# Two layers of an SSM convolution and a GEGLU FFN: another order of passes, half visits at the handover, and block 1's transform by tokens mod 4

## The chip, the cores and the metric

The kernel runs on one core of a Trainium2 chip. The metric is the device time of one execution in microseconds, and less is better. In the names below PE is the matmul engine (TensorE), DVE the VectorE, ACT the ScalarE, POOL the GpSimd and SP the SyncE, whose queue issues most DMAs; PEld are PE's weight loads.

## The reference

```python
def _A_ref(q, k, v, shift_k, ssm_k, ssm_D):          # B=1, S=2048, D=576
    k_shift = sum over t<4 of k_pad[:, t:t+S, :] * shift_k[:, 3-t]
    kv = k_shift * v
    y  = causal convolution of kv with ssm_k along S   # rfft of length 2S in the reference
    return q * (y + kv * ssm_D)

def _B_ref(x, w_gate, w_up, w_down):                  # F=4608
    return (_gelu(x @ w_gate) * (x @ w_up)) @ w_down

x = A_q
x = x + _A_ref(_layernorm(x), A_k, A_v, A_shift_k, A_ssm_k, A_ssm_D)
x = x + _B_ref(_layernorm(x), B_w_gate, B_w_up, B_w_down)
x = x + _A_ref(_layernorm(x), A_k, A_v, A_shift_k, A_ssm_k, A_ssm_D)
x = x + _B_ref(_layernorm(x), B_w_gate, B_w_up, B_w_down)
```

Two layers share all weights. The convolution works on `k` and `v` alone, so its result `y` is the same in both layers; only the gate `q` differs.

## The kernel before

**Units, passes, visits.** The 2048 tokens are four chunks of 512 (`CH`), a chunk four rows of 128 tokens. A unit is one layer of one chunk, numbered 0 to 7: (0,0), (0,1), (1,0), (1,1), (0,2), (0,3), (1,2), (1,3), as (layer, chunk). `passes` (L810) lists which units go through the FFN together. A pass runs three phases `ph` (`NP`), each over 12 of the 36 tiles of 128 features, and in each phase visits its units in turn, so that the units of a pass share one load of the weights. A visit of a unit has two parts. First, for each of 12 tiles, 18 matmuls `gu` (L1103): nine blocks of 64 rows of the contraction, `gate` weights on the upper half of PE's rows and `up` weights on the lower half, 512 columns each. Then the `down` product `dn` (L1768), 192 matmuls of 64 rows and 288 columns that add four rows of tokens, two rows at a time (`two_rows`).

**Evictions.** A tile's PSUM bank is emptied in one of two ways: ACT does the gelu (L1700) and DVE multiplies it with `up` from PSUM (L1701); or, when there is much work for DVE, ACT does the gelu (L1691) and a copy of `up` (L1692), and DVE multiplies the two from SBUF (L1693). The product is `hT`, which `dn` reads. Three PSUM banks go round among `gu` and `dn` tiles; the fourth, `cps`, belongs to the convolution, which may borrow one of the three.

**Handover.** After the last phase of a unit in layer 1 each row goes through a chain: sum into `x_c` with the row's total (L1798), mean on POOL (L933), sum of squares on ACT (L941), `rstd` on POOL (L949), the factor `yh` from `y` on ACT (L977), the gate on DVE (L987), again mean, squares and `rstd`, the norm `xn` on DVE (L1016, L1018), and two DMA transposes on SP (L1058) into `xnT`, the moving operand of the next unit's `gu`.

**The convolution.** Class `Conv` transforms blocks of 512 tokens of `kv` and of the filter, multiplies them (`prod`) and transforms back (`inverse`) into `y[m]`, needed by chunk m. Blocks 2 and 3 are transformed in quarters, by tokens mod 4 (`fwd4`, `quarter`, 288-column matmuls `cps` at L310); block 1 by `fwd` and `fwd_h`, with twice as many matmuls. These are put between the matmuls of the FFN.

**Order.** The order of every engine is fixed when the program is built. A planner (`Pace` with the costs `C_..`, `fill`, `run_v`, `run_vq`, `run_aq`, `run_p`) keeps an estimate of each engine's clock and fills the convolution and the handover in beside the visits' work. Weights are loaded by SP in its program order: `load_wgu` (L869 to L877, three DMAs for one set of four tiles; three buffers) and `load_wd` (L879 to L885; three buffers). `when_due` gives each a due time, and `weights` issues it up to `SOON` = 30 us ahead, but only `HOLD` = 14 us ahead while rows wait for their norm or transposes. A load waits on SP until its buffer has been read, and what stands behind it waits too.

Of the kernel before, what the change touches and what calls it, by code (L numbers as in the profile page):

```python
# [10 lines left out]
ACT = mybir.ActivationFunctionType  # L11
# [22 lines left out]
C_P0, C_P1, C_AC = 1.28, 1.35, 0.7  # L34
C_TT, C_ST, C_BN, C_NORM, C_HT, C_GELU, C_EVA, C_EVD, C_YH = 0.74, 0.80, 0.47, 0.62, 0.615, 0.51, 0.56, 0.72, 0.7
C_HB = 0.345
C_FOLD = 0.46
# [3 lines left out]
SLOW, PRESS = 5.0, 22.0  # L41
# [93 lines left out]
class Conv:  # L135
# [9 lines left out]
    def __init__(self, tc, ctx, pace, gwork, xtp, A_k, A_v, A_shift_k, A_ssm_k, A_ssm_D, ident, cps, ypool):  # L145
# [22 lines left out]
        self.nT = self.cst.tile([P, 5, P], BF16, name="nT")  # L168
        self.V_ = self.cst.tile([P, 2, RT, P], BF16, name="V")
        self.nV = self.cst.tile([P, 3, P], BF16, name="nV")  # L170
# [124 lines left out]
    def fwd_eo(self, src, kt, s, h, ring, scale=1.0):  # L295

        nc = self.nc
        ps = yield from self.both_steps(lambda ps: [ps[:, e, 0:HW] for e in range(2)],
                                   [([self.fw(kt, s, i + e) for e in range(2)],
                                     [src(i + e)[:, h * HW:(h + 1) * HW] for e in range(2)]) for i in (0, 2)])  # L300
        eo = self.eo_tile(ring)
        nc.scalar.activation(out=eo[:], in_=ps[:, :, 0:HW], func=ACT.Copy, scale=scale)
        return eo

# [16 lines left out]
    def quarter(self, src, e, s, h, scale=1.0):  # L321
# [5 lines left out]
        eo = self.eop.tile([P, 2, HW], F32, tag="eo", name="eo")  # L327
# [3 lines left out]
    def cross(self, eo, lo, hi):  # L331
        for dst, op in ((lo, ALU.add), (hi, ALU.subtract)):
            self.nc.vector.tensor_tensor(out=dst, in0=eo[:, 0, :], in1=eo[:, 1, :], op=op)

# [59 lines left out]
    def step(self, m, kv=None, loaded=False):  # L394
# [74 lines left out]
        def fwd(kt, s, h):  # L469
            def run():  # L470
                if s == 0 and h == 0:
                    for k in (kt, kt + 2):
                        kc[k] = self.kcp.tile([P, 2, D], BF16, tag="kc", name="kc")
                free, ring = self.eo_free(True)
                self.eo_at[ring].popleft()
                cur = self.cur
                eo = yield from self.fwd_eo(lambda i: self.vt_[m][:, i, :], kt, s, h, ring)
                done = t.on_act(C_EVA, max(t.pe + 0.25 + LAG, free))
                self.ps_free[cur] = done
                if (kt, s, h) == (1, 1, 1):  # L480
                    self.fwd_at[m] = t.pe + 0.25
                cols = slice(h * HW, (h + 1) * HW)

                def fin():
                    self.cross(eo, kc[kt][:, s, cols], kc[kt + 2][:, s, cols])
                    when = t.on_dve(2 * C_BF, done + LAG)
                    self.eo_at[ring].append(when + LAG)
                    mark(("kc", kt, s, h), when + LAG)
                    if s == 1 and h == 1 and m < self.NB - 1:
                        for k in (kt, kt + 2):  # L490
                            self.spill(self.Kd[m][k], kc[k], when + LAG)
                self.U.append((done + LAG, 2 * C_BF, fin))
            return run

        hh = self.hh if m == 1 else {}

        def fwd_h(kt, s, h):
            def run():
                if (kt, s, h) == (0, 0, 0):
                    self.hh_tiles()  # L500
                free, ring = self.eo_free(True)
                self.eo_at[ring].popleft()
                cur = self.cur
                eo = yield from self.fwd_eo(self.ht[m], kt, s, h, ring, 1.0 / NFQ)
                done = t.on_act(C_EVA, max(t.pe + 0.25 + LAG, free))
                self.ps_free[cur] = done
                if (kt, s, h) == (1, 1, 1):
                    self.hf_at[m] = t.pe + 0.25
# [1361 lines left out]
```

## Time and profile before

| | before |
|---|---|
| median of 3 runs | 909.99 us (909.66 to 910.07) |
| span of the profiled execution (no device time of its own is listed for it) | 907.9 us |
| what the median has beyond that span | 2.1 us |
| PE busy | 902.9 us, 99% of the span |
| DVE, ACT, POOL busy | 556.8, 364.5, 142.0 us |
| DMA | 129.73 MB, mean 143 GB/s |

The profile is one execution, taken by the hardware profiler. Its page gives busy times and shares; a busy PE says little, since matmuls are pipelined and their ends modelled. The chain that ended last is followed back from the last instruction, step by step to what released it. A group of instructions has one row: its line, engine, operation, tile written <- tiles read, shapes and count, then busy us and mean ns, then the idle time before. A DMA's landing is counted from its issue. In a table by stretches of time, the columns after PE, PEld, DVE, ACT and POOL are PE's granted clock, the mean busy share of the DMA engines, and GB/s.

### The profile page before, as it was taken

How to read it: one execution, taken by the hardware profiler on the slowest of the kernel's cores; microseconds unless marked ns; L12 is line 12 of the kernel's file. 1: busy time of each engine (PE TensorE's matmuls, PEld its weight loads, DVE VectorE, ACT ScalarE, POOL GpSimd, SP SyncE). 2: the span in 40 equal slices, each digit the busy share in tenths (PEclk: the TensorE clock that was granted, in tenths of full speed). 3: DMA queues.
4: the chain of work that ended last, by engine and by line, in shares of the span. 5: the costliest groups of instructions: out<-in, count | busy, mean ns of one | idle time of the engine just before them, and what ended most of it. 6: DMA issues, size and time to landing. Idle time of an engine off the chain costs nothing.

```text
span 907.9 us, 24267 instructions
## 1 busy us (share of the span) xinstructions
PE 902.9 (99%) x10465; PEld 601.3 (66%) x10465; DVE 556.8 (61%) x1109; ACT 364.5 (40%) x677; POOL 142.0 (16%) x311
## 2 busy tenths in 40 slices
PE   9999999999999999999999999999999999999998
PEld 7757656577576675775766766757757657667666
DVE  8898988654789876667888744553333334433332
ACT  7784446625434356354244233451121224321211
POOL 5423003320113012230023001220000002100000
PEclk9999999999999999999999999999999999999999
DMA  9999967877519503974934702762720820777630
GB/s 242 314 265 285 231 143 137 179 232 135 170 56 258 128 3 67 270 201 102 251 120 123 167 14 69 138 124 63 136 79 3 157 80 14 142 178 179 135 102 28
DMA packets 128272, 129.73 MB, mean 143 GB/s; under 512 B 43298, under 2 KB 120483, under 8 KB 128164
## 3 DMA queue, kind: packets, MB, share of 16 engines
q1 hardware_dynamic: 119138, 93.22, 47.7%
q0 software_dynamic: 8880, 34.36, 11.0%
q8 instruction: 82, 1.34, 0.6%
q10 hardware_dynamic: 146, 0.59, 0.2%
q14 instruction: 26, 0.21, 0.1%
HBM read 106.91 MB, written 11.80 MB: 131 GB/s over the span
## 4 chain that ended last, share of the span: by engine, by line
PE 98%; POOL 0%; ACT 0%; issue 0%; DVE 0%; ACTq 0%
PE gu L1103 61%; PE dn L1768 30%; PE cps L310 2%; PE ps L284 2%; PE dn L1729 1%; PE ps L1344 0%; PE ps L1103 0%; PE ps L1479 0%; POOL rstd L1564 0%; PE ps L1257 0%; PE ps L1315 0%; PE cps L373 0%; PE ps L278 0%; ACT yh L1526 0%; PE ps L1373 0%
## 5 line engine op out<-in xcount | busy, mean ns | idle before, releaser
L1103 PE MATMUL gu<-xnT,wgu 64*128 64x512 bf16 x5148 | 561.4, 376 | 0.0
L1103 PEld LDWEIGHTS <-wgu 64*128 64x128 bf16 x5220 | 293.2, 94 | 260.6 <-issue 0.7
L1768 PE MATMUL dn<-wd,hT 64*128 64x288 bf16 x4512 | 293.9, 283 | 0.0
L1768 PEld LDWEIGHTS <-hT 64*128 64x128 bf16 x4512 | 254.4, 94 | 26.2
L1700 ACT ACTIVATE ga<-gu 128x512 f32<-128x512 f32 x175 | 104.4, 597 | 311.0 <-PE gu L1103 307.8
L1701 DVE TENSOR_TENSOR hT<-ga,gu 128x512 bf16<-128x512 f32 x175 | 120.1, 687 | 167.5 <-ACT ga L1700 167.3
L1691 ACT ACTIVATE ga<-gu 128x512 bf16<-128x512 f32 x111 | 66.2, 597 | 149.9 <-PE gu L1103 143.9
L1693 DVE TENSOR_TENSOR hT<-ga 128x512 bf16<-128x512 bf16 x112 | 47.0, 421 | 59.6 <-ACT ga L1692 59.5
L1692 ACT CAST ga<-gu 128x512 bf16<-128x512 f32 x111 | 64.3, 579 | 0.0
L933 POOL TENSOR_SCALAR means<-s 128x1 f32<-128x1 f32 x28 | 10.4, 372 | 248.7 <-DVE x_c L1798 219.4
L1804 DVE SCALAR_TENSOR_TENSOR x_c<-dn,means,x_c 128x576 f32<-128x576 f32 x28 | 22.8, 815 | 28.4 <-PE dn L1768 28.4
L1806 DVE TENSOR_TENSOR x_c<-x_c,dn 128x576 f32<-128x576 f32 x32 | 24.1, 752 | 25.8 <-PE dn L1768 25.5
L949 POOL TENSOR_TENSOR rstd<-ve,neghalf_t 128x1 f32<-128x1 f32 x56 | 35.4, 632 | 4.7
L345 DVE TENSOR_TENSOR prod<-prod 128x576 bf16<-128x576 bf16 x64 | 29.3, 458 | 2.2
L328 ACT ACTIVATE eo<-cps 128x576 f32<-128x576 f32 x32 | 20.8, 651 | 23.5 <-PE cps L310 17.3
L1785 DVE TENSOR_TENSOR xn<-x_c,dn 128x576 bf16<-128x576 f32 x15 | 11.3, 754 | 26.5 <-PE dn L1768 24.2
L656 DVE TENSOR_TENSOR kc<-ab,cd 128x288 bf16<-128x288 f32 x64 | 25.3, 452 | 0.0
L443 POOL DMA_DIRECT2D kr<-Kd x20 | 11.2, 558 | 88.2 <-DVE prod L344 88.2
L941 ACT ACTIVATE junk<-x_c,nm 128x576 bf16<-128x576 f32 x28 | 21.5, 769 | 2.2 <-POOL nm L933 1.6
L977 ACT ACTIVATE yh<-y,rstd 128x576 f32<-128x576 bf16 x28 | 21.4, 768 | 1.1 <-POOL rstd L949 1.1
L448 POOL DMA_DIRECT2D hr<-Hd x32 | 17.8, 556 | 24.1 <-DVE prod L344 22.6
L948 POOL TENSOR_SCALAR ve<-ss 128x1 f32<-128x1 f32 x56 | 13.9, 248 | 43.7 <-ACT junk L941 43.4
(177 smaller groups left out, 626.4 us busy)
## 6 DMA issues: line engine op xcount, KB each, us to landing
wgu<-in_B_w_gate_dram SPq DMA_DIRECT2D x45, 576.0 KB, 5.9
wd<-in_B_w_down_dram SPq DMA_DIRECT2D x30, 864.0 KB, 7.1
wgu<-in_B_w_up_dram SPq DMA_DIRECT2D x45, 512.0 KB, 7.5
hr<-Hd POOLq DMA_DIRECT2D x32, 288.0 KB, 4.6
kr<-Kd POOLq DMA_DIRECT2D x24, 288.0 KB, 3.9
Kd<-kc POOLq DMA_DIRECT2D x12, 288.0 KB, 6.4
k<-in_A_k_dram POOLq DMA_DIRECT2D x3, 1008.0 KB, 10.3
wgu<-in_B_w_up_dram SPq DMA_DIRECT2D x45, 64.0 KB, 7.3
```

The source lines that it names most:

```text
L345: nc.vector.tensor_tensor(out=dst[:, cols], in0=pr[:, 0, cols], in1=pr[:, 1, cols], op=ALU.subtract if part == 0 else ALU.add)
L656: nc.vector.tensor_tensor(out=into[k][:, plane, cols], in0=a, in1=b, op=op)
L949: nc.gpsimd.tensor_tensor(out=v["rstd"][:], in0=ve[:], in1=neghalf_t[:, 0:1], op=ALU.pow)
L1103: nc.tensor.matmul(cols(pair[:, s, :]), lhsT=w[r0:r0 + HK, k, gi * P:(gi + 1) * P], rhs=cols(xnT[r0:r0 + HK, blk_of[k], :]), start=(k == 0 ...
L1691: nc.scalar.activation(out=ga[:, 0, :], in_=pair[:, 0, :], func=ACT.Gelu_apprx_tanh)
L1692: nc.scalar.copy(out=ga[:, 1, :], in_=pair[:, 1, :])
L1693: nc.vector.tensor_tensor(out=hT[:, fi, :], in0=ga[:, 0, :], in1=ga[:, 1, :], op=ALU.mult)
L1700: nc.scalar.activation(out=ga[:], in_=pair[:, 0, :], func=ACT.Gelu_apprx_tanh)
L1701: nc.vector.tensor_tensor(out=hT[:, fi, :], in0=ga[:], in1=pair[:, 1, :], op=ALU.mult)
L1768: nc.tensor.matmul(acc[:, g, 0:HW], lhsT=lhs[r], rhs=wn[r, g * HW:(g + 1) * HW], start=step == 0 and fi == 0, stop=step == 1 and fi == FP - 1)
L1804: nc.vector.scalar_tensor_tensor(out=xh, in0=acc[:, :, 0:HW], scalar=m_[:, 0:1], in1=xh, op0=op, op1=ALU.add)
L1806: nc.vector.tensor_tensor(out=xh, in0=xh, in1=acc[:, :, 0:HW], op=ALU.add)
```

## The change

Passes go `[0], [2], [1], [3, 4], [5, 6], [7]` in place of `[0], [1, 2], [3, 4], [5, 6], [7]`: chunk 0 does both its layers first, then chunk 1 alone does layer 1, then its layer 2 with chunk 2. That makes six passes of three phases, so the weights are loaded six times and not five. The last visit of layer 1 and the first of layer 2 of chunks 0 and 1 (`SPLIT`) are done in halves of 256 tokens: 12 tiles of `gu` with 256 columns, the `dn` of two rows, then the same for the other two rows. The first half of the layer-2 visit needs only two rows of `xnT`. Block 1 goes through `fwd4` like the other blocks, on both rings of `eo` tiles; `fwd`, `fwd_h` and `fwd_eo` are gone. The products of the convolution are split into multiplications and a later `join`. Square sums write to one persistent `junk`, the negated planes `nT`, `nV` go to a pool of the start, transposes may be issued up to `SPREAD` = 2 us ahead of the planned norm, and the preparation of a row moves to other visits.

```diff
-    passes = [[0], [1, 2], [3, 4], [5, 6], [7]]
+    passes = [[0], [2], [1], [3, 4], [5, 6], [7]]
     NWB = len(passes) * NP
+    at_once = [units.index((1, c)) for c in range(2)]
+    SPLIT = {(units.index((0, c)), NP - 1) for c in range(2)} | {(n, 0) for n in at_once}
...
+        if ui in at_once:
+            return tasks + [norm(i) for i in range(j - 1, j + 1) if j % 2]
         lag = 2 if layer == 0 else 1
...
     def spreads(now=False, tensor=False):
-        while xn_made and (now or xn_made[0][3] <= t.pe):
+        while xn_made and (now or xn_made[0][3] <= t.pe + (SPREAD if xn_made[0][0] == coming[0] and t.pe > due_at[0] - PRESS else 0.0)):
...
-            if conv_first:
+            if conv_first and not pressing():
...
-        at_start = {(0, 0): [("es", 1), ("prep", 1)], (1, 0): [("x", 2)], (2, 1): [("es", 2)],
+        at_start = {(0, 0): [("es", 1)], (2, 1): [("prep", 1)], (1, 0): [("x", 2)], (1, 1): [("es", 2)],
...
+            split = (ui, ph) in SPLIT
...
+            inputs(RT // 2 if split else RT)
...
+            def features(part=None):
+                ahead[0] = NEVER
+                conv.alt = None
+                last = final and part != 0
+                size = 1.0 if part is None else 0.5
+                cols = (lambda a: a) if part is None else (lambda a: a[:, part * CH // 2:(part + 1) * CH // 2])
...
+                for fi in range(FP):
+                    n, gi = divmod(wb * FP + fi, FG)
+                    w = wgu[n]
...
+                        pair = pr("gu")
+                        gu(pair, w, gi, cols, xnT)
...
+                    if gi == FG - 1 and last:
+                        when_due(t.pe + (FP - FG) * C_GU + 12.0, load_wgu, n + 3)
...
+            for part in range(2) if split else (None,):
+                if part == 1:
+                    inputs(RT)
+                if part != 0:
+                    begin()
...
+                features(part)
...
+                for j in (0, 2) if part is None else (2 * part,):
+                    rows(j)
...
         def steps(filt, ready):
-            limit = lambda: max(ready(), 0.0 if self.eo_at["eo"] else NEVER)
-            if m > 1:
-                for h in range(2):
-                    for e in range(2):
-                        for s in range(2):
-                            self.Pq.append((limit, 0.25, fwd4(filt, e, s, h)))
-                return
-            for kt in range(2):
-                for s in range(2):
-                    for h in range(2):
-                        self.Pq.append((lambda: max(
-                            ready(), 0.0 if self.eo_at["eo"] or self.eo_at["yh"] else NEVER), 0.49, (fwd_h if filt else fwd)(kt, s, h)))
+            limit = lambda: max(ready(), 0.0 if self.eo_at["eo"] or m == 1 and self.eo_at["yh"] else NEVER)
+            for h in range(2):
+                for e in range(2):
+                    for s in range(2):
+                        self.Pq.append((limit, 0.25, fwd4(filt, e, s, h)))
...
+    def mul(self, part, K, H, pr):
+        nc = self.nc
+        if part == 0:
+            nc.vector.tensor_tensor(out=pr[:], in0=K[:], in1=H[:], op=ALU.mult)
+        else:
+            for s in range(2):
+                nc.vector.tensor_tensor(out=pr[:, s, :], in0=K[:, s, :], in1=H[:, 1 - s, :], op=ALU.mult)
+
+    def join(self, part, pr, dst):
+        self.nc.vector.tensor_tensor(out=dst, in0=pr[:, 0, :], in1=pr[:, 1, :], op=ALU.subtract if part == 0 else ALU.add)
...
+        def products(kt, items):
...
+            steps = [(ready(items[n][0]), C_M1 if items[n][1] else C_M0, mult(n)) for n in reversed(range(len(items)))]
+            return steps, (now, len(items) * C_BF + 0.02, join)
```

More of the change, by code (lines that the diff above doesn't have):

```diff
@@ L40 @@
 AHEAD = 2.0
-SLOW, PRESS = 5.0, 22.0
+SLOW, PRESS, SPREAD = 5.0, 22.0, 2.0
 NAT, NEAR = 22.0, 2.2
@@ L467, in step @@
                            load(kt, a)))
[L469 to L493, printed above, removed]
@@ L542, in fin, with join @@
                         if a < m:
                             self.kr_free[kr[(kt, a)][0]] = when
-                return fin
-            return run
+                    return fin
+                return run
+            def join():
+                for n in reversed(range(len(items))):
+                    a, part = items[n]
+                    dst = hr[(kt, a)][1][:, part, :] if own else tiles[len(items) - 1][:, n, :]
+                    self.join(part, tiles[n], dst)
+                    prs[part, a, kt] = dst
+                return lambda when: None
```

297 lines of the change are left out of this document (144 added, 153 removed).

## The prediction

> **What bounds the kernel now.** I read the page's busy shares first, then the chain that ended last, then that chain in order of time.
>
> ```profile
> PE 902.9 (99%) x10465; PEld 601.3 (66%) x10465; DVE 556.8 (61%) x1109; ACT 364.5 (40%) x677; POOL 142.0 (16%) x311
> DVE  8898988654789876667888744553333334433332
> PEclk9999999999999999999999999999999999999999
> PE 98%; POOL 0%; ACT 0%; issue 0%; DVE 0%; ACTq 0%
> ```
>
> A busy PE alone proves little, because matmul ends are modelled. The chain does: 98% of the span is PE released by PE, at full clock. In order of time it gives unit prices:
>
> ```profile
> core 0 of [0], span 907.9 us
> ...
> 40.09 3.05 PE ps L1103 x54
> 43.39 0.98 PE ps L1103 x18
> 44.37 0.49 PE cps L310 x8
> 83.23 23.31 PE gu L1103 x216
> 106.54 11.76 PE dn L1768 x192
> 333.81 1.71 PE dn L1768 x28
> 335.77 0.78 ACT yh L977
> 336.63 0.66 ACT eo L328
> 337.33 0.30 PE cps L310 x2
> ```
>
> A full visit is 216 `gu` matmuls in 23.31 us (107.9 ns each, 512 columns) and 192 `dn` in 11.76 (61.25 ns each, 288 columns): 35.07 us; 24 of them are 841.7. A half-row `cps` matmul of the convolution costs the same as a `dn`: 8 in 0.49. After 40.09 the chain has only one real wait: from 333.81 + 1.71 = 335.5 to 337.3 it runs over ACT (`yh`, and `eo` queued behind it), and the `cps` matmuls around it are worth 0.1 us. So a matmul that goes away is gained in full, a wait of PE is lost in full, and all that waiting could give back is under 2 us. The span is 907.9, the median of the runs 910.0: 2.1 us lie around the span and are added at the end.
>
> **The change part by part.** Counts and orders of instructions are those of the two built programs.
>
> *Block 1 by tokens mod 4.* The forward matmuls on `cps` go from 256 to 192, all 64 of them block 1's (128 to 64); the 64 half-row and 16 full inverse ones stay. They lie on PE's chain: 64 x 61.25 ns = **-3.9 us**. DVE gets 32 more operations of 288 columns and has the rest regrouped.
>
> ```profile
> L656 DVE TENSOR_TENSOR kc<-ab,cd 128x288 bf16<-128x288 f32 x64 | 25.3, 452 | 0.0
> ```
>
> 32 x 0.45 = 14 us of DVE at most, where DVE is 50 to 90% busy; block 1 is due three visits (105 us) later than before, so PE's own work covers it: 0, and if the cover went, PE would wait for those 14 us at visit 6.
>
> *Halves.* Four visits (last of layer 1, first of layer 2, chunks 0 and 1) do 1728 `gu` matmuls of 256 columns in place of 864 of 512. The only rows at 256 columns are the early ones above: 56.5 ns (54 in 3.05, with the start of the stage in it) and 54.4 (18 in 0.98, one tile in steady flow), against 107.9 / 2 = 53.95: +0.8 to +4.4 us. I take the steady row: **+0.9**. [...]
>
> *The wait at 335 us* hangs on ACT's order around one `cps` slot. That order is new, so I let it go: **-1.8** (between -1.8 and 0).
>
> *Order of passes.* Layer 2 of a chunk follows its layer 1 at once, so the chain from a row's `dn` to its `xnT` (sum, square, root, `yh`, gate, square, root, norm, two transposes) now has one half visit of time. Its prices, and those of the evictions that share ACT and DVE with it:
>
> ```profile
> L1700 ACT ACTIVATE ga<-gu 128x512 f32<-128x512 f32 x175 | 104.4, 597 | 311.0 <-PE gu L1103 307.8
> L1701 DVE TENSOR_TENSOR hT<-ga,gu 128x512 bf16<-128x512 f32 x175 | 120.1, 687 | 167.5 <-ACT ga L1700 167.3
> L328 ACT ACTIVATE eo<-cps 128x576 f32<-128x576 f32 x32 | 20.8, 651 | 23.5 <-PE cps L310 17.3 <-PE dn L1768 3.1 <-DVE cd L333 2.9
> L941 ACT ACTIVATE junk<-x_c,nm 128x576 bf16<-128x576 f32 x28 | 21.5, 769 | 2.2 <-POOL nm L933 1.6 <-DVE hT L1701 0.4
> L977 ACT ACTIVATE yh<-y,rstd 128x576 f32<-128x576 bf16 x28 | 21.4, 768 | 1.1 <-POOL rstd L949 1.1
> L1016 DVE TENSOR_SCALAR xn<-x_c,nm,rstd 128x576 bf16<-128x576 f32 x28 | 16.1, 576 | 1.5 <-POOL rstd L949 1.5
> L1018 DVE COPY xn<-xn 128x64 bf16<-128x64 bf16 x28 | 5.1, 182 | 1.0
> ...
> L1058 SPq DMA_TRANSPOSE xnT<-xn x56: 1200/1257/2270, 142.2 to 786.1; - x56
> ```
>
> No row has a 128x256 eviction. On ACT its bounds are half and all of the 128x512 one, 0.30 and 0.60; 64 more columns cost 54 ns (597 to 651), so 256 fewer some 0.2, and I take 0.40. On DVE 0.34 to 0.69, and by the same thought 0.42. T0 is the end of the first half's `dn` in visit 2. The second half has 12 tiles of 0.98 (11.75) and 96 `dn` (5.88), so visit 3 would start at T0 + 17.6. In that half ACT has 18 evictions, two `yh` and four squares: 18 x 0.40 + 6 x 0.77 = 11.8 of 11.75 us, just full. The third tile ends at T0 + 2.95, but `yh` and a square stand before its eviction (2.9 to 4.45); DVE is through with it at 5.3, and its bank is due for the sixth tile at 4.9: 0.5 us late. Visit 8 has the like: **+1.0** in all (0 to 3). The ninth tile ends at 9.3, ACT's two evictions of it at 10.35, DVE's product at 10.65; then come the two rows' norms, 0.76 each, done at 11.4 and 12.2. Their four transposes take SP 1.25 each, from 11.4 to 16.4.
>
> **What stands behind them on SP comes late.** The new order of SP is: first `wgu` of visit 3 (after tile 4), the four transposes, second `wgu`, a `wd`, third `wgu`, a `wd`. The second buffer is free at T0 + 7.8, but its load is queued behind transposes that wait for `xn`. The same pattern, and a quieter one, in whole visits of before:
>
> ```profile
> 580.63 0.63 SPq L874 DMA_DIRECT2D wgu<-in_B_w_gate_dram  x1
> 581.31 0.63 SPq L875 DMA_DIRECT2D wgu<-in_B_w_up_dram  x1
> 583.35 0.64 SPq L875 DMA_DIRECT2D wgu<-in_B_w_up_dram  x1
> 787.51 0.60 SPq L874 DMA_DIRECT2D wgu<-in_B_w_gate_dram  x1
> 788.16 0.64 SPq L875 DMA_DIRECT2D wgu<-in_B_w_up_dram  x1
> 790.21 0.64 SPq L875 DMA_DIRECT2D wgu<-in_B_w_up_dram  x1
> ...
> DMA to landing us min/median/max: 8.6/8.6/8.6
> DMA to landing us min/median/max: 10.5/11.1/11.7
> DMA to landing us min/median/max: 5.5/6.5/7.4
> DMA to landing us min/median/max: 10.7/10.7/10.7
> ...
> 587.00:589.00 2.00, 2.00 (x36) 1.84 (x34) 1.59 (x5) 1.29 (x3) 0.73 (x2) 1.00 1.15 207
> 162.00:166.00 4.00, 4.00 (x42) 2.07 (x38) 3.91 (x9) 2.82 (x7) 2.48 (x6) 1.00 1.06 362
> ...
> DMA to landing us min/median/max: 2.5/2.6/5.2
> ...
> wgu<-in_B_w_gate_dram SPq DMA_DIRECT2D x45, 576.0 KB, 5.9
> wd<-in_B_w_down_dram SPq DMA_DIRECT2D x30, 864.0 KB, 7.1
> wgu<-in_B_w_up_dram SPq DMA_DIRECT2D x45, 512.0 KB, 7.5
> ...
> wgu<-in_B_w_up_dram SPq DMA_DIRECT2D x45, 64.0 KB, 7.3
> ```
>
> The first four landing rows are those of the `up` loads at 581.31, 583.35, 788.16 and 790.21, in this order, the largest value each (the smaller ones are `gate` parts); the fifth is that of all transposes. From the first issue on, the first load is there after 9.3 and 8.0 us (581.31 + 8.6 - 580.63; 788.16 + 7.4 - 787.51), the second after 14.4 and 13.4. With only `wgu` in flight the DMA moves 207 GB/s at a share above 1; where `wd` lands, 362. A set of `wgu` is 576 + 512 + 64 = 1152 KB, a `wd` 864: between two sets it adds 2.4 to 4.2 us.
>
> *Visit 3.* Second `wgu`: issued at T0 + 16.4, there at 24.4 to 25.7; due for the fifth tile at 17.6 + 0.5 + 3.9 = 22.0. Third: there at 16.4 + (13.4 to 14.4) + (2.4 to 4.2) = 32.2 to 35.0, due for the ninth at 26.0. PE loses the larger lateness, 6.2 to 9.0; if the norms came right behind the ninth tile and all of it 1.9 us sooner, 4.3. I take **+6.5**, near the quiet pair, since little else is in flight there. The `wd` behind are then due after T0 + 36 and come in the same stream.
>
> *Visit 9* (layer 2 of chunk 1). Here the third `wgu` stands ahead of the `wd`, 16 `cps` matmuls make the visit start at T0 + 18.6, and the second norm ends at 12.8, so SP is free at 15.6. Second: there at 23.6 to 24.9, due 22.5. Third: 29.0 to 30.0, due 26.5. **+2.9** (1.4 to 3.6).
>
> Elsewhere the loads have a whole visit, or, in the second half of visit 3, no transposes before them. Start-up to 40 us has the same order on every engine.
>
> Sum: -3.9 + 0.9 - 1.8 + 1.0 + 6.5 + 2.9 = +5.6. 907.9 + 5.6 + 2.1 = **915.6 us**.
>
> **The rivals.**
>
> *A, weights in time (faster).* Without both late loads: 915.6 - 9.4 = 906.2. SP would have to be free by about T0 + 9, or loads in a row land within some 6 us each. For it: the least of those landings, 5.5 us for a `gate` part. Against it: no norm can stand before the ninth tile's product, and four transposes are 5 us. Chance 0.15.
>
> *B, a faster transfer (no change).* At 362 GB/s for all three loads of visit 3, after some 2.5 us of latency, the third is there at 16.4 + 2.5 + 3168 / 362 = 27.7, due 26.0: 1.7 us, and nothing at visit 9: 907.9 us. [...] Chance 0.13.
>
> *C, ACT bounds the halves (slower still).* At 0.60 per eviction a tile that ACT evicts wholly takes 1.2 us against 0.98, and 52 tiles are so: +10 us, 925.6, with norms and loads later as well. It decides from 0.49 on. The 54 ns for 64 columns speak against it. Chance 0.10.
>
> That the change does not do what it says (the rows of the handover late all the same) is near: the last transpose, started at T0 + 15.2 with the row's usual 2.6 us to land, is there at 17.8 against 18.1. A microsecond more costs one per handover, within the 0 to 3 above.
>
> **How the numbers follow.** The forecast holds 0.62, its own range 911 to 920. The range 905.5 to 922 reaches to A and B and takes in the upper ends of the terms; C lies above it. A measurement of this kernel can tell about 0.2%, 1.8 us: faster is below 908.2, slower above 911.8. Faster: A and a part of B, 0.18. Same: the rest of B and the lowest part of the forecast, 0.14. Slower: 0.68.
>
> **What would show it.** 192 forward `cps` matmuls; 1728 `gu` of 256 columns at 54 to 56 ns each; in the chain, DMA or idle PE ahead of `gu` near 154 to 163 us and 380 to 390 us, together some 9 us, with SP's transposes just ahead of the late loads; 128x256 evictions near 0.40 us on ACT. Wrong would be: no wait for `wgu` at visit 3 (A), loads in a row within 6 us (B), evictions of 0.5 and more (C), or a wait in a place that I hold to be covered.

## The result, and the profile after

| | before | after |
|---|---|---|
| median | 909.85 us (909.66 to 910.07, 4 runs) | 950.53 us (949.17 to 953.87, 4 runs) |
| ratio, 95% interval | | 1.0453 (1.0435 to 1.0471) |
| span of the profiled execution | 907.9 us | 947.3 us |
| PE busy, mean granted clock | 902.9 us, 1.000 | 914.6 us, 0.987 |

Slower, as forecast, but by 40.7 us and not by 5.6. From the page of the changed kernel, the rows that answer to those of before (busy times, then the slices, then the chain's shares):

```profile
PE 914.6 (97%) x11265; PEld 584.0 (62%) x11265; DVE 569.5 (60%) x1190; ACT 371.9 (39%) x749; POOL 143.4 (15%) x311
PE   9999998899899999977999999999999999999998
PEclk9999999999999999989999999999999999999999
PE 90%; DMA 5%; DVE 2%; SPq 1%; ACT 1%; issue 1%; POOL 1%; ACTq 0%; POOLq 0%; DVEq 0%
```

PE fell from 98% of the chain to 90%; DMA, DVE and SP's queue took its place. The spans differ by 39.4 us: PE is busy 11.7 us longer, though it has 64 forward matmuls fewer, and idle 32.7 us in place of 5.0 (span less busy). What PE waited for after its start-up:

```profile
PE gu L1081 <- DMA wgu<-in_B_w_up_dram: 11.1, 5, 2.4
PE gu L1081 <- DMA xnT<-xn: 10.1, 4, 5.1
PE gu L1081 <- DMA wgu<-in_B_w_gate_dram: 3.9, 3, 1.9
PE gu L1081 <- issue: 1.1, 1, 1.1
PE gu L1081 <- DVE x_c L1806: 0.7, 1, 0.7
```

(us in total, times, longest.) Weights 15.0 us, rows 10.1. To see where, both spans are cut at the starts of visits 3, 6, 9 and 12; the table by stretches, limited to the convolution's `cps` matmuls of half rows, shows the length, their busy time and number, the same of their weight loads, then the mean clock, the DMA's busy share and GB/s. First before, then after:

```profile
40.09:157.29 117.20, 15.14 (x152) 8.21 (x152) 1.00 0.89 214
157.29:265.14 107.85, 6.03 (x40) 2.63 (x40) 1.00 0.62 159
265.14:374.54 109.40, 8.05 (x64) 3.86 (x64) 1.00 0.54 122
374.54:481.89 107.35, 4.82 (x32) 2.12 (x32) 1.00 0.68 183
```

```profile
40.09:152.17 112.08, 8.01 (x64) 3.84 (x64) 1.00 0.88 204
152.17:281.80 129.63, 9.13 (x64) 3.88 (x64) 0.96 0.95 202
281.80:392.60 110.80, 9.41 (x76) 4.19 (x76) 1.00 0.81 198
392.60:521.31 128.71, 3.48 (x20) 1.58 (x20) 0.95 0.71 164
```

The differences are -5.1, +21.8, +1.4 and +21.4 us: the two stretches that begin with a handover cost 21 to 22 us each, with a clock of 0.96 and 0.95. The first gains what left it, 88 half-row matmuls. PE's timeline names the waits: `wgu` at visit 3 (157.5 to 168.8: 1.33 + 2.33 + 0.64 + 2.20 = **6.5**), `wgu` at the start of visit 5 (1.93 + 2.22 = **4.1**), `wgu` at visit 9 (1.97 + 2.40 = **4.4**), and rows: the second half of visit 9 and the start of visit 10.

```profile
157.51 0.28 PE L1081 MATMUL gu<-xnT,wgu 64*128 64x256 bf16 x1 [1.33 <-DMA wgu<-in_B_w_gate_dram]
160.12 5.53 PE L1081 MATMUL gu<-xnT,wgu 64*128 64x256 bf16 x71 [2.33 <-DMA wgu<-in_B_w_up_dram]
...
244.75 2.54 PE L1081 MATMUL gu<-xnT,wgu 64*128 64x512 bf16 x12 [2.22 <-DMA wgu<-in_B_w_up_dram]
...
405.79 5.57 PE L1081 MATMUL gu<-xnT,wgu 64*128 64x256 bf16 x71 [2.40 <-DMA wgu<-in_B_w_up_dram]
...
422.25 0.28 PE L1081 MATMUL gu<-xnT,wgu 64*128 64x256 bf16 x2 [4.15 <-DMA xnT<-xn]
...
447.99 0.61 PE L1081 MATMUL gu<-xnT,wgu 64*128 64x512 bf16 x2 [5.07 <-DMA xnT<-xn]
```

The second and fourth rows also show another part of the loss: 71 matmuls of 256 columns take 5.53 and 5.57 us, 78 ns each in place of 54. By stretches of 2 us the clock behind the wait of 2.40 us is:

```profile
406.00:408.00 2.00, 2.00 (x22) 1.47 (x20) 0.00 (x0) 0.08 (x1) 0.00 (x0) 0.50 1.09 355
408.00:410.00 2.00, 2.00 (x34) 1.62 (x31) 1.25 (x4) 1.44 (x4) 0.78 (x3) 0.79 0.63 201
410.00:412.00 2.00, 2.00 (x40) 1.78 (x36) 1.14 (x4) 1.25 (x4) 2.00 (x4) 1.00 0.73 116
```

In finer steps the clock is halved from 405.42 us, still within the wait, to 408.83: 3.41 us. There are six such stretches after 40 us, five of 3.41 us and one, at visit 10, of 6.83. Over the span, 1 - 0.987 is 12.3 us of full clock; a part of it falls into the waits themselves, where it costs nothing. In the 3.41 us up to 405.42 PE was busy for 1.32 us, 39%; the last section has the same for all six.

SP's queue around these waits is as the prediction read it from the order of instructions:

```profile
145.08 5.83 SPq L1036 DMA_TRANSPOSE xnT<-xn  x4
151.00 0.60 SPq L852 DMA_DIRECT2D wgu<-in_B_w_gate_dram  x1
...
155.36 1.94 SPq L853 DMA_DIRECT2D wgu<-in_B_w_up_dram  x1
...
217.34 18.26 SPq L1036 DMA_TRANSPOSE xnT<-xn  x8
235.70 0.62 SPq L852 DMA_DIRECT2D wgu<-in_B_w_gate_dram  x1
```

The second set of visit 3 goes out behind four transposes (SP is through with them 16.6 us after the end of the first half's `dn` at 134.3; 16.4 were forecast), and the first set of visit 5 behind eight, which wait for norms for 18 us and which no PE work needs before visit 6.

### The profile page after: what moved, and what is told of

It is laid out like the page before. It is cut to its first block, busy times and chain, and to the rows that moved or that the text cites. A ratio compares the mean times of both kernels' runs of the same rounds, so it can differ in the third digit from the quotient of the medians.

```text
span 947.3 us, 26081 instructions
## 1 busy us (share of the span) xinstructions
PE 914.6 (97%) x11265; PEld 584.0 (62%) x11265; DVE 569.5 (60%) x1190; ACT 371.9 (39%) x749; POOL 143.4 (15%) x311
## 4 chain that ended last, share of the span: by engine, by line
PE 90%; DMA 5%; DVE 2%; SPq 1%; ACT 1%; issue 1%; POOL 1%; ACTq 0%; POOLq 0%; DVEq 0%
PE gu L1081 58%; PE dn L1768 26%; DMA wgu<-in_B_w_up_dram 4%; PE ps L283 1%; PE cps L299 1%; DMA xnT<-xn 1%; SPq L1036 1%; PE dn L1729 1%; DVE kc L635 1%; PE ps L1324 0%; DVE cd L322 0%; PE ps L1459 0%; PE ps L1081 0%; PE ps L1235 0%; POOL rstd L1543 0%
## 5 line engine op out<-in xcount | busy, mean ns | idle before, releaser
L1081 PE MATMUL gu<-xnT,wgu 64*128 64x512 bf16 (+1 forms) x6012 | 577.7, 350 | 27.9 <-DMA wgu<-in_B_w_up_dram 11.1
L1081 PEld LDWEIGHTS <-wgu 64*128 64x128 bf16 x6084 | 307.4, 95 | 288.8 <-issue 18.6
L1768 PEld LDWEIGHTS <-hT 64*128 64x128 bf16 x4512 | 227.5, 94 | 52.7 <-issue 0.7
L1702 DVE TENSOR_TENSOR hT<-ga,gu 128x512 bf16<-128x512 f32 (+1 forms) x198 | 123.9, 627 | 197.4 <-ACT ga L1701 197.2
L1701 ACT ACTIVATE ga<-gu 128x512 f32<-128x512 f32 (+1 forms) x198 | 108.4, 549 | 299.7 <-PE gu L1081 299.3
L1692 ACT ACTIVATE ga<-gu 128x512 bf16<-128x512 f32 (+1 forms) x136 | 70.1, 516 | 145.8 <-PE gu L1081 124.6
L1694 DVE TENSOR_TENSOR hT<-ga 128x512 bf16<-128x512 bf16 (+1 forms) x137 | 50.4, 370 | 55.1 <-ACT ga L1693 54.6
L1693 ACT CAST ga<-gu 128x512 bf16<-128x512 f32 (+1 forms) x136 | 67.7, 498 | 0.0
L917 ACT ACTIVATE junk<-x_c,means 128x576 bf16<-128x576 f32 x16 | 12.3, 772 | 27.4 <-POOL means L910 25.2
L322 DVE TENSOR_TENSOR ab<-eo 128x288 f32<-128x288 f32 x48 | 19.3, 451 | 5.5 <-ACT eo L317 3.5
```

The source lines that it names most:

```text
L917: nc.scalar.activation(out=junk[:], in_=get_x(), func=ACT.Square, bias=v["nm"][:, 0:1], accum_out=v["ss"][:])
L1081: nc.tensor.matmul(cols(pair[:, s, :]), lhsT=w[r0:r0 + HK, k, gi * P:(gi + 1) * P], rhs=cols(xnT[r0:r0 + HK, blk_of[k], :]), start=(k == 0 ...
L1692: nc.scalar.activation(out=cols(ga[:, 0, :]), in_=cols(pair[:, 0, :]), func=ACT.Gelu_apprx_tanh)
L1693: nc.scalar.copy(out=cols(ga[:, 1, :]), in_=cols(pair[:, 1, :]))
L1694: nc.vector.tensor_tensor(out=cols(hT[:, fi, :]), in0=cols(ga[:, 0, :]), in1=cols(ga[:, 1, :]), op=ALU.mult)
L1701: nc.scalar.activation(out=cols(ga[:]), in_=cols(pair[:, 0, :]), func=ACT.Gelu_apprx_tanh)
```

## The experiments

All times are medians beside runs of the kernel before on the same chip (909.7 to 909.8 us each time); ratios are to it.

### Block 1 alone, and the first theory

My first theory, T, was the order on SP, two late `xnT` and the half clock. Rivals: R1, half visits cost time by themselves; R2, six loads of all weights are too many; R3, the regrouped block 1.

**e1_old_passes**

```diff
-    passes = [[0], [2], [1], [3, 4], [5, 6], [7]]
+    passes = [[0], [1, 2], [3, 4], [5, 6], [7]]
...
-    SPLIT = {(units.index((0, c)), NP - 1) for c in range(2)} | {(n, 0) for n in at_once}
+    SPLIT = set()
```

(`at_once` empty, `at_start` as before.)

> Block 1 by tokens mod 4 and the regrouped products alone; the order of passes and the whole visits are those of before. My theory (T: the loss of 40 us is weight sets queued on SP behind the handover's transposes, two late xnT, and half clock after each of these waits) expects nothing of it here: 64 forward matmuls fewer at 61 ns are -3.9 us, up to -1.8 more if the wait at 335 us goes: 904.2 to 906.5 us. Rival R3 (the regrouped block 1 with its 32 more operations of DVE makes PE wait) expects 910 or more, with waits of PE on DVE or ACT in visits 3 to 8.

Measured: **910.93 us**, 1.0015 (1.0006 to 1.0023). T's figure was wrong, R3's right. PE's waits in this kernel:

```profile
PE cps L1097 <- DVE xn L992: 1.9, 2, 1.2
...
PE gu L1081 <- DVE ab L322: 0.7, 1, 0.7
```

Visit 1 starts at 79.3 us against 83.0, so the 3.7 us are there; at visit 3, with 157.4 against 157.1, they are gone. The four evictions of chunk 1's `y` end at 142.8 us (before: 136.0) and its last `xn` at 152.7 (147.2); PE waits 2.8 us at 148 to 158 and turns two rows itself (18 matmuls with the identity, 1.4 us). Why `y` is later with fewer matmuls was not looked into. In these runs, then, block 1 by tokens mod 4 saves its matmuls only where block 1 is due later, as in the new order of passes.

**e2_whole_visits** (the changed kernel with `SPLIT` and `at_once` empty)

> The new order of passes with all visits whole. A row's transposes then end only after the visit's last dn, and PE waits for the chain from there (sum, square, root, yh, gate, square, root, norm, transposes: some 8 to 12 us by the rows of after) at visits 3 and 9; but SP has no transposes in front of the weight sets of visits 3 and 9, so those waits (6.5 + 4.4 + 4.6 us) go, and 4 half-clock stretches of 1.7 us with them, while visit 5's and visit 10's stay. T expects the two to balance: 950.5 - 0.9 - 15.5 - 6.8 + 2 x (10 + 1.7) = 951 us, 943 to 960, with no wait for wgu at visit 3 or 9. Rival R1 (the half visits themselves cost the time) expects all of the 36 us back but the two handovers of some 12 us: 930 to 935 us.

Measured: **947.55 us**, 1.0421 (1.0405 to 1.0437). As T expected: the `wgu` waits of visits 3 and 9 are gone (only 2.9 us are left, at visit 5), and 21.3 us of waiting for rows on DVE and ACT stand in their place. Whole visits come out 3 us better than halves, where R1 wanted 15 to 20: R1 is out as the main cause.

**e3_hold30**

```diff
-HOLD, SOON, QUIET, LEAD, FAR = 14.0, 30.0, 10.0, 1.8, 3.6
+HOLD, SOON, QUIET, LEAD, FAR = 30.0, 30.0, 10.0, 1.8, 3.6
```

> The changed kernel, with weight loads issued as soon as their buffer is free and no longer held back 14 us ahead of their due time while transposes are near: SP has one more set ahead of the transposes of visits 3, 5 and 9, and the later sets still stand between or behind them. T expects the waits at visit 3 to fall from 6.5 to 0 to 3 us, at visit 5 from 4.1 to 0 to 1, at visit 9 from 4.4 to 0 to 1, and 3 to 5 stretches of half clock at 1.7 us each to go; the xnT waits of 4.6 and 5.5 us stay: 950.5 - 12 - 7 = 931 us, 926 to 938. Rival R1 (half visits) and rival R2 (six loads of the weights in place of five: the transfer itself is too slow) expect 946 to 952.

Measured: **955.93 us** (952.32 to 960.52; the profile is of the last), 1.0510 (1.0477 to 1.0544): slower, where T had 931. **T falls.** The order on SP did change, and the waits for weights shrank, but the waits for rows grew:

```profile
PE gu L1081 <- DMA xnT<-xn: 28.9, 7, 11.6
PE dn L1768 <- DMA wd<-in_B_w_down_dram: 6.2, 1, 6.2
PE gu L1081 <- DMA wgu<-in_B_w_up_dram: 2.0, 1, 2.0
```

**e4_pool_queue** (HOLD = 30, and `load_wgu` takes `nc.gpsimd.dma_start` for sets 10, 11, 15, 16, 17, 28 and 29)

> As the last one, and the seven sets that stood behind transposes (two of visit 3, three of visit 5, two of visit 9) are issued by POOL, whose rows have 0.55 us for one issue, in place of SP. T expects that no set is late any more: 950.5 - (6.5 + 4.1 + 4.4) - 5 x 1.7 = 927 us, 922 to 934, with the xnT waits of visits 9 and 10 left over; if POOL's own waits (its hr and kr loads wait for DVE) hold a set back, one wait for wgu stays and costs 2 to 5 us. R1 and R2 expect 946 to 952: the same bytes move in the same halves.

Measured: **984.14 us**, 1.0824 (1.0806 to 1.0842), with 33.6 us of waiting for `xnT`. The reason is in the DMA issues between 130 and 160 us (KB each, median us from issue to landing). First after, then the kernel with HOLD = 30, then this one:

```profile
xnT<-xn SPq DMA_TRANSPOSE x4, 2.6
```

```profile
xnT<-xn SPq DMA_TRANSPOSE x4, 6.3
```

```profile
wgu<-in_B_w_gate_dram POOLq DMA_DIRECT2D x2, 576.0 KB, 9.6
wgu<-in_B_w_up_dram POOLq DMA_DIRECT2D x2, 512.0 KB, 11.5
...
xnT<-xn SPq DMA_TRANSPOSE x4, 11.7
```

The same four transposes take 2.6 us to land where SP's last load was issued 4.8 us ahead of them, 6.3 with one set more ahead of them on SP, 11.7 with two sets on POOL's queue, the first issued from 142.9 us, ahead of them, and the second from 146.7, beside them. Another issuing queue gave them no way around the loads here. From here on the theory was **T2**: a handover has to move the rows' transposes and the next visit's sets through the same DMA engines within half a visit; whichever goes second is late.

### Taking DMA out of the handover

**e10_turn_on_pe**

```diff
     def spreads(now=False, tensor=False):
...
+            if xn_made[0][0] in at_once and not now:
+                if not tensor or conv.ps_free[0] > t.pe:
+                    return
+                turn_row(*xn_made.popleft())
+                continue
...
-                    if split and xn_made and xn_made[0][3] <= t.pe:
-                        spreads()
-                    elif not split and xn_made and xn_made[0][3] - 0.3 <= t.pe:
+                    if xn_made and xn_made[0][3] - 0.3 <= t.pe:
                         turn_row(*xn_made.popleft())
```

(And rows of these units no longer hold the loads back.)

> The changed kernel with the 16 transposes of the two handovers taken off SP and the DMA queues: PE turns those 8 rows (9 matmuls with the identity per row), ACT or DVE evicts them, and the weight sets no longer wait for them. New theory T2 (in a handover the rows' transposes and the next visit's weight sets share the DMA queues, which hold about 200 GB/s of wgu; whichever is issued second is late, so an order on SP cannot help, only less DMA) expects: the wgu waits of visit 3 and of visit 9 (6.5 + 4.4 us) and the xnT wait inside visit 9 (4.6) go, with 4 stretches of half clock (1.7 each); PE does 72 more matmuls of 76 ns (5.5 us) and waits 0 to 2 us at each of four half visits for a row; visit 5's and visit 10's waits stay. 950.5 - 15.5 - 6.8 + 5.5 + 4 = 938 us, 932 to 943. If weight loads are too slow by themselves (R2: six loads of all weights, 5.2 MB per 35 us visit in visits 3 to 8), visits 3 and 9 keep waits for wgu and it stays above 945.

Measured: **939.40 us**, 1.0327 (1.0311 to 1.0342), in T2's range. Visit 3 waits 1.0 us for `wgu` in place of 6.5; visit 9 keeps 3.4 of 4.4; its second half no longer waits for its rows. Visit 5 (6.2 us) and visit 10 (4.4) wait on, and 1.6 us for a row's `x_c` on DVE are new.

**e11_no_loads**

```diff
+    KEPT = (3, 5, 9)
...
+        if n // GP in KEPT:
+            wgu[n] = wgu[n - GP]
+            return
```

> The changed kernel without the nine wgu loads of visits 3, 5 and 9: these visits multiply with the sets of the visit before them, so that part of the computation is changed and its loads are left out; every transpose, instruction of PE and handover stays. T2 expects the transposes of the handovers to land in 2.5 to 3.5 us and no wait in visit 3, at the start of visit 5 or in the first half of visit 9: 950.5 - (6.5 + 4.1 + 4.4) - 5 x 1.7 = 927 us, 923 to 931; the xnT waits of 4.6 us in visit 9 and 5.5 at visit 10 stay. Rival R4 (the handover's chain over DVE, ACT and POOL is itself too long for half a visit) expects the waits to turn into waits for xnT at visits 3 and 9: 935 to 945. R1 (the half visits cost it) expects 945 or more.

Measured: **929.77 us**, 1.0218 (1.0203 to 1.0233), also T2's range. Not one wait is left in visits 3 and 5 and in the first half of visit 9; the transposes of visit 3 land in 2.6 us. So at visit 3 the chain over DVE, ACT and POOL fits into half a visit: R4 is out there, and so is R1, since the half visits are all still in. What stays:

```profile
PE gu L1085 <- DMA xnT<-xn: 12.7, 4, 7.4
```

stands at the second half of visit 9 (7.4 + 0.4) and at visit 10 (4.5 + 0.4); their causes are below.

### What the half clock costs

**e5_warm**

```diff
+    WARM = {(2, 0, 0, 4): 60, (2, 0, 0, 8): 45, (1, 0, None, 0): 75, (3, 0, 0, 4): 30, (3, 0, 0, 8): 45, (3, 0, 1, 0): 75, (4, 0, None, 0): 95}
...
                         pair = pr("gu")
+                        for _ in range(WARM.get((ui, ph, part, fi), 0)):
+                            nc.tensor.matmul(pair[:, 0, 0:P], lhsT=ident[:], rhs=ident[:], start=True, stop=True)
                         gu(pair, w, gi, cols, xnT)
```

> The changed kernel with 425 extra matmuls of PE (identity by identity, 128 columns, into the bank that the next tile overwrites from its start) ahead of the seven tiles that wait longest, about as many as the waits are long: they add work that nothing uses. If the granted clock of 0.50 for some 3.4 us behind each wait comes from PE's idling, it stays at 1.0 and the 1.7 us of each of five waits and the 3.4 us at visit 10 come back: 950.5 - 11.9 = 938.6 us, 935 to 942, while the same transfers land at the same times. If the half clock comes from elsewhere, nothing is gained: 949 to 953, or more where the extra matmuls outlast the waits.

Measured: **953.76 us**, 1.0478 (1.0461 to 1.0495): a miss. The mean clock rose from 0.987 to 0.995, but 75 matmuls had been placed at visit 6, where nothing waits, visit 5's wait was left open, and in visit 3 the saved time came back as a longer wait for the third set.

**e5b_warm** (406 such matmuls, only at the last wait of each series)

> As the first kernel with extra matmuls, now placed only at the last wait of each series (visit 3 tile 9, the start of visit 5, visit 9 tile 9, the second half of visit 9, the start of visit 10; 406 in all, identity by identity, results overwritten): the first placed 75 of them at visit 6, where nothing waits, and left visit 5's wait open. A transfer lands when it lands, so time that a full clock saves ahead of a later wait is given back in it; only what lies behind the last wait of a series comes back: 1.7 us at visit 3, 1.7 at visit 5, 1.7 to 3.4 at visit 10: 944 us, 941 to 948, with a mean clock of 0.995 or more. If the half clock does not matter at all, or the matmuls outlast the waits: 949 to 954.

Measured: **946.81 us** (943.98 to 954.00), 1.0396 (1.0380 to 1.0412), mean clock 0.994 to 0.998. With PE kept busy in these waits most of the half clock was gone: by these clocks 6.6 to 10.4 of the 12.3 us are back, but the median fell by 3.7 only. The rest seems to lie ahead of a later wait, where a faster PE waits longer for the same transfer: in the profile, which is of the slowest run, visit 9's last set has 3.5 us of wait behind 48 extra matmuls, 2.4 in after.

### The rivals by themselves

**e8_six_passes** (`passes = [[0], [1], [2], [3, 4], [5, 6], [7]]`, else as e1)

> The kernel of the first experiment (910.9 us: block 1 by tokens mod 4 in the old order) with its pass of two units cut in two: six loads of all weights in place of five, visits 3 to 5 for chunk 1 layer 1 and 6 to 8 for chunk 0 layer 2, all whole, and no handover inside a visit. T2 expects only the one set that stands behind transposes at visit 6 to be late: 911 to 917 us. R2 (the weights of a pass of one unit, 5.2 MB per visit, come too slowly whatever stands around them) expects waits for wgu or wd in visits 3 to 8 and 920 to 930 us.

Measured: **916.94 us** (910.88 to 918.75), 1.0067 (1.0045 to 1.0089). One set is late, at visit 4 and not at visit 6 as I wrote: the third one, issued at 192.2 us behind transposes that hold SP from 180.4 to 192.1. Its last part lands 21.1 us after its issue, as the chain has it, beside loads of `wd`, `kr`, `hr` and `v`; so the order on SP and the fuller DMA may both have a share in it.

```profile
PE gu L1081 <- DMA wgu<-in_B_w_up_dram: 2.5, 1, 2.5
...
PE gu L1081 <- DMA wgu<-in_B_w_gate_dram: 1.9, 1, 1.9
```

Two of the nine runs took 910.9 and 911.6 us at a clock of 1.000, so the set is not late every time. Six loads without a tight handover cost 6 us over e1 in the median, not 40: R2 by itself is a small part.

**e6_halves_old** (as e1, with `SPLIT = {(n, 1) for n in range(4)}`)

> The kernel of the first experiment (910.9 us) with four visits cut in halves of 256 tokens that hand nothing over: the middle third of the weights of the first four units, so 1728 matmuls of 256 columns in place of 864 of 512, and the shorter evictions, with no row that is waited for. Mine: 1728 x 54.4 - 864 x 107.9 ns = +0.8 us, and up to 1.5 more where loads or evictions shift: 911.7 us, 910.5 to 914. R1 (half visits cost time by themselves, by matmul, eviction or bank) expects 915 to 950, and waits of PE on ACT or DVE inside these visits.

Measured: **915.25 us**, 1.0072 (1.0051 to 1.0093): 4.3 us over e1, more than I expected and less than R1 wants. The half matmuls by themselves:

```profile
L1081 PE MATMUL gu<-xnT,wgu 64*128 64x256 bf16 x1728 | 96.2, 269 | 0.3
```

96.2 / 1728 = 55.7 ns of PE each; 864 whole ones at 561.4 / 5148 = 109.1 ns (the group's row of before, 561.4 us for 5148) would be 94.2, so +2.0 us and not +0.9. The chain of this run agrees, with 216 half ones in 11.97 us (55.4 ns each) where 216 whole ones take 23.31: +2.5 for four visits. The rest is a `wgu` wait of 1.6 us at visit 2 and one more row turned on PE (0.7).

### The rows that are late at visits 9 and 10, and what is left

**e13_loads_behind** (the convolution's first four pairs of block 3, `kr` and `hr`, on SP behind the four transposes of visit 9, in place of POOL, and planned no sooner than 17 us after the first half of visit 9 is begun)

> The changed kernel with the convolution's seven loads (288 KB each, kr and hr) that start 0.5 us behind the four transposes in visit 9 moved from POOL's queue to SP's, behind these transposes. T2 expects the four transposes to land in 2.5 to 4 us each in place of 5.7 and the xnT wait of the second half of visit 9 to fall from 4.6 us to 0 to 1.5; visit 10 takes some of it back, since its rows then stand behind seven more issues on SP (0.6 us each): 950.5 - 3.8 - 1.7 + 2 = 947 us, 943 to 950. If the transposes of visit 9 are late by their norms and not by the DMA queues, the wait stays at 4 to 5 us and the time at 949 to 954.

Measured: **945.00 us** (942.72 to 950.15; the profile is of the last), 1.0394 (1.0368 to 1.0421). The transposes land in 2.7 us (median of the eight issued between 375 and 430 us; 3.8 in after), and the second half of visit 9 no longer waits for them (4.6 us in after); visit 10 still waits 5.3. In this run the waits for `wgu` are 19.6 us in place of 15.0, some of it at visits 3 and 5, which the edit does not touch: the profile shows the cause of the one wait, and its time is not a clean price.

**e12_turn_early** (e10; loads of visit 5 not held back for rows due at visit 6; and the preparation of chunk 2 layer 1 begins in the first half of visit 9)

```diff
                 while late:
                     add_late()
+                if part == 0 and (ui, ph) == (3, 0):
+                    begin()
...
-                if part != 0:
+                if part != 0 and (ui, ph) != (3, 0):
                     begin()
```

> The kernel that turns the handover's rows on PE (939.4 us), with two repairs: at visit 5 the weight sets are no longer held back behind the eight transposes of chunk 1 layer 1, which are due a visit later; and the preparation of chunk 2 layer 1, due at visit 10, starts in the first half of visit 9 in place of the second. T2 expects visit 5's wait (4.2 + 2.1 us) to fall to 0 to 1.5 and visit 10's (4.4) to 0 to 2, with 1.7 us of half clock behind each: 939.4 - 5.5 - 3.5 - 3.4 = 927 us, 922 to 932; visit 9's wgu wait of 3.4 stays. If the loads of one-unit passes are too slow wherever they are issued, a wait for wgu or wd of 2 us or more comes back in visits 5 to 8: 932 to 938.

Measured: **930.35 us**, 1.0225 (1.0212 to 1.0239). Visit 10's wait of 4.4 us is down to 0.3: its rows had simply been begun too late. At visit 5 the first set is now in time, but the third waits 0.9 + 2.3 us and a `wd` 1.7: one repair passed the wait on. That a visit's 5.2 MB in a pass of one unit keep the DMA too full for more is argued here; the next run bears it out.

**e16_both** (e12 without the nine loads of visits 3, 5 and 9, as in e11)

> The kernel with rows turned on PE and the two repairs (930.4 us), without the nine wgu loads of visits 3, 5 and 9, which multiply with the sets of the visit before: that part of the computation is changed. What T2 lays to the loads of one-unit passes goes: waits of 1.4, 0.9 + 2.3, 1.7 (wd) and 2.4 us, and some 4 us of half clock: 930.4 - 8.7 - 3 = 919 us, 914 to 923; what stays are the PE transposes (5.5), rows waited for on DVE (3) and half visits (1 to 2), against 906 for the forward matmuls saved and nothing else. If waits for rows take the place of those for weights, 924 to 930.

Measured: **919.91 us**, 1.0108 (1.0091 to 1.0125). With the loads gone, rows are in time: PE waits for no DMA, 3.0 us for `x_c` on DVE at the start of halves and visits, and 1.6 for its own issue. So 10.4 us of e12 are these loads. Of the 10.2 us that stay over before, turning (5.5), `x_c` (3.0), issue (1.6) and half visits (2.0) less block 1 (3.9) make 8.2.

**e14_five_turn** (only chunk 0's handover is tight, turned on PE as in e10; five loads; `at_once` is unit 2 alone, `SPLIT` its first visit and unit 0's last, and two preparations move to other visits)

```diff
+    passes = [[0], [2, 1], [3, 4], [5, 6], [7]]
...
-                       for ph in range(NP) for k, ui in enumerate(us)]
+                       for ph in range(NP) for k, ui in enumerate(us if (pi, ph) != (1, NP - 1) else us[::-1])]
```

> Only what block 1 needs of the new order, with the weights of both layers still shared: chunk 0 layer 2 and chunk 1 layer 1 in one pass of two units (five loads of all weights as before), chunk 0 layer 2 first in the first two thirds and last in the last one, so only visit 3 has a tight handover (half visits, rows turned on PE), and chunk 1 layer 1 is due one visit later than before in place of three. T2 expects one tight handover's price: against 910.9 us of block 1 by tokens mod 4 alone, its late rows of chunk 1 (2.8 us of waits and 1.4 of turning) go, and the handover's wait for wgu (1 us) and for a row (1.6), the turning of four rows (2.7), two half visits (1 to 2) and 1.7 of half clock come: 915 us, 911 to 919. If the new position of chunk 1 layer 1 or the rest of the changed schedule costs it, 925 or more.

Measured: **922.86 us**, 1.0144 (1.0129 to 1.0160): a miss by 8 us. The handover itself waits as expected (1.8 for `wgu`, 1.6 for a row), but visit 4 waits for the rows of chunk 1:

```profile
PE gu L1086 <- DMA xnT<-xn: 4.7, 2, 4.1
PE gu L1086 <- DMA wgu<-in_B_w_up_dram: 1.8, 1, 1.8
PE gu L1086 <- DVE x_c L1807: 1.6, 1, 1.6
```

**e15_five_dma** (the same with DMA transposes)

> The same with the four rows of the handover transposed by DMA, as in the changed kernel. T2 expects the wgu waits of visit 3 as there (6.5 us, two stretches of half clock of which 1.7 us counts) in place of PE's turning and the 2.6 us of waits: 915 - 5.3 - 1.7 + 8.2 = 917 us, and 0 to 4 more where the sets of visit 5 stand behind twelve transposes: 914 to 922. If the transposes by DMA cost nothing against PE's, 911 to 914.

Measured: **928.31 us**, 1.0202 (1.0186 to 1.0217). The same wait at visit 4 (5.7 us) lifts it too. By DMA the one tight handover costs 5.4 us more than by PE, where I had 2, with the `wgu` waits of visit 3 back at 6.3 us.

**e17_five_early** (e14 with the preparation of chunk 1 layer 1 begun in the first half of visit 3)

> The kernel with shared weights and one tight handover turned on PE (922.9 us), whose second unit's preparation starts in the first half of visit 3 in place of the second half; there PE waited 4.15 + 0.54 us at visit 4 for that unit's rows. If the late start of the preparation is the cause, the wait falls to 0 to 1.5 us and one stretch of half clock (1.7) goes with it: 922.9 - 4 - 1.7 = 917 us, 915 to 920. If the rows are late by DVE, ACT or the DMA queues, wherever their preparation starts, it stays at 921 to 925.

Measured: **923.71 us**, 1.0151 (1.0134 to 1.0168): no gain, the wait stays at 5.2. Here the start of the preparation was not the cause. The last `y` row of block 1 leaves `cps` on DVE at 176.7 us in this kernel, and the chain from there, with evictions in between, ends in the last `xn` at 194.4; the first `yh` starts right behind ACT's first `y` of that time (174.3). By this order block 1 is still too late; whether its work could be planned sooner there was not tried.

None of these beats the kernel before; the nearest is e1, with the old order.

## Why the prediction was wrong

The step that failed is the one that put at nothing all that lies outside the two late sets. The span grew by 39.4 us, and 5.6 were forecast. Of the 33.8 between, the half clock behind the waits is up to 12.3, late rows 10.1, late sets at visit 5 4.1, and visit 9's sets 1.5 more than forecast.

- **Direction and first mechanism: right.** `wgu` late behind the transposes at visit 3: 6.5 us forecast, 6.5 measured, with SP free at T0 + 16.6. That the two figures are the same is in part luck: the third set landed at T0 + 34.4 (168.7), 8.4 us behind its due time of T0 + 26.0, and PE waited only 6.5 of them because it had lost some 1.7 before at half clock (71 matmuls in 5.53 us). At visit 9: 2.9 forecast, 4.4 measured.
- **"Elsewhere the loads have a whole visit": wrong at visit 5.** Its sets stand behind eight transposes that wait for norms over 18 us (4.1 us of wait). I had looked only at the two tight handovers.
- **The rows were taken as in time** ("That the change does not do what it says ... is near", 0 to 3 us). They cost 10.1 us: in the second half of visit 9 the transposes land in 5.7 us beside seven loads, and PE does not wait for them where these loads stand behind them (e13), and visit 10's preparation starts half a visit later, since `begin` is called in the second part (e12).
- **A wait of PE was costed at its length.** With each of the six waits of 2 us and more in after (2.20 to 5.07) came a stretch of half clock, of 3.41 us or twice that. 12.3 us of clock are missing, of which only some 4 came back with the transfers as they are (e5b). No row of before could show it: it has no such wait after 40 us.
- **A price that was right for a reason too narrow.** I read SP's order as the cause. Turning it around (e3, e4) made it worse: with more loads ahead of them or beside them the transposes of visit 3 landed in 6.3 and 11.7 us, and I had used the row of 2.6 for one in the midst of loads.
- **Block 1, -3.9**: the 64 matmuls went (the groups have 96 and 96 on `v` and `ht` in place of 128 and 128), and visit 1 starts 3.7 us earlier. **Halves, +0.9**: 2.0 to 2.5 (e6); the term was mis-sized, 54.4 ns from one tile where the steady price is 55.4 to 55.7. **Banks and ACT, +1.0**: 0.3 us of waiting on `hT` in after; evictions of 256 columns took 0.38 us on ACT and 0.42 on DVE, forecast 0.40 and 0.42. **The wait at 335 us, -1.8**: gone, with 0.7 us for `x_c` at visit 8 in its place.
- **The rivals**: B's 362 GB/s did not come (at visit 3 the third set landed at T0 + 34.4, where B had 27.7, or 27.9 with KB of 1024 bytes, and from 244 to 250 us, where `wgu` lands at visit 5, the DMA moves 201), nor C's slow evictions; A was wrong for all three late visits.
- **The range** had no case for a second DMA stream in a handover or for the clock. The terms of after, roughly: waits +27.7, clock +12.3, halves +2.0, block 1 -3.9, together +38 of the span's 39.4.

What stays open: the 1.1 us at 122 us that PE's waits put down to issue, why e1's `y` comes later than before, and how its block 1 could be ready for chunk 1 in the old order.

## What to carry to other kernels

When a change removes the slack between a producer and its consumer, list all that must cross the DMA engines in the new gap and price it as one stream: in e3 and e4 another order on SP and another queue made the rows late (28.9 and 33.6 us of waiting for `xnT`, 10.1 in after); then look for the same pattern in every visit whose neighbours changed, not only at the seam. Price a wait of PE of 2 us and more with the half clock that came with each such wait in after (3.41 us at 0.50 lose 1.7), but only the last wait of a series: in e5b 6.6 to 10.4 us of clock came back and the median fell by 3.7. Work taken off the bound engine counts only if what it produced is not needed sooner than it is now ready: e1 has 64 matmuls fewer and a ratio of 1.0015.

## What the runs showed of the hardware

- The transposes of 128 rows of visit 3 landed 2.6 us after their issue in after, where SP's last load was issued 4.8 us ahead of them, 6.3 us (median of four) in e3 with one `wgu` set more (1152 KB) ahead of them on SP, and 11.7 in e4 with two sets on POOL's queue.
- In after the granted clock is 0.50 in six stretches after 40 us. They begin at 159.66, 169.90, 244.99, 405.42, 422.49 and 446.38 us, the later five 3, 25, 72, 77 and 84 times 3.413 us behind the first; each lasts 3.41 us, the sixth 6.83. In the 3.41 us ahead of each of them PE was busy for 8, 35, 18, 39, 7 and 0%. Around the fourth, PE alone (length, PE busy, clock, DMA share, GB/s):

```profile
395.18:398.59 3.41, 1.80 (x33) 1.00 1.13 204
398.59:402.01 3.42, 3.06 (x56) 1.00 1.14 202
402.01:405.42 3.41, 1.32 (x20) 1.00 1.11 228
405.42:408.83 3.41, 3.04 (x30) 0.50 1.08 354
```

- A wait of some 2 us did not always bring half clock. In after the wait of 2.40 us at visit 9 did, with PE busy for 1.32 of the 3.41 us (39%), and the one of 1.97 before it did not, with 1.80 (53%). In e12 two waits at visit 5, of 0.9 and 2.3 us with one matmul between them, left the clock at 1.00 (all engines):

```profile
250.00:253.00 3.00, 1.98 (x17) 0.68 (x12) 2.21 (x7) 1.84 (x4) 0.38 (x1) 1.00 1.13 197
253.00:255.20 2.20, 0.04 (x2) 0.04 (x4) 0.77 (x3) 0.00 (x0) 1.77 (x4) 1.00 1.11 206
255.20:257.00 1.80, 1.80 (x18) 0.85 (x20) 0.00 (x0) 0.00 (x0) 0.00 (x0) 1.00 1.08 356
```

- Some of the kernels that wait on DMA repeat less well: the runs of e5b spread over 1.1% and those of e13 over 0.8%, those of before over 0.05%; those of e14, which waits too, over 0.1%.
